# A long convolution with a mixture of experts: when the rows are ranked and scattered

## The chip, the cores and the metric

The kernel runs on one core of a Trainium2 chip. The metric is the device time of one execution in microseconds, as the median of the runs. One further execution was profiled; rows of the profile are from that one.

## The reference

The program first convolves and then routes. For each of 4 batches of 10048 rows with 128 channels:

```python
h_filt = (np.maximum(pos_emb @ w1, 0.0) @ w2) * window
y = irfft(rfft(x * v, n=2 * S) * rfft(h_filt, n=2 * S))[:, :S]
x = (x * y).reshape(B * S, D)          # 40192 rows of 128
```

Each row then chooses one of 4 groups (the largest of `x @ w_group`) and one of 4 experts in it (the largest of `x @ w_expert[g]`). It goes through that expert alone, with the product of the two softmax weights as its factor:

```python
out[row] = g_w * e_w * (np.maximum(x[row] @ w1[g, e], 0.0) @ w2[g, e])
```

## The kernel before

The convolution is a discrete Fourier transform written as matrix products on TensorE (PE). For batch `b` there are two stages.

- The *way in* forms `x * v`, folds it (`product`, `fold`, on VectorE) and transforms it in 43 steps of three channels (`dft_blocks`, matmuls `psa`, evicted to `z` by ScalarE). Between these steps stand the inverse transforms of the batch before (`turned`, `inverse_blocks`: matmuls `pt` and `po`, evictions `tt` and `oo` on ScalarE, `yt` and `xy` on VectorE).
- The *middle* runs over 40 pairs of frequencies. Each step is a matmul `psb` (`dft_positions`), the product with the filter's spectrum (two VectorE operations `t`, L629 and L632, then two halves of `y` on GpSimd, L630 and L633), and five steps later a matmul `pbp` from `y` back into `z` (`back`, evicted by ScalarE, L648).

W1, W2, W3 are the ways in of batches 1 to 3, each with the inverse of the batch before; M1, M2, M3 are the middles that follow them. A last way in holds the inverse of batch 3 alone. After it comes the experts' stage (`moe`).

What was convolved is routed meanwhile. `conv` drives a generator `routing` with `next(routing, None)`: 22 pieces of `chosen` (transpose rows, multiply by the router's weights, choose), then the pieces of `ranked`, which count the rows of each expert and compute a place `adr` in a sorted table `prow` for each row. In M1 batch 0 is chosen and its ranking begins, and so on. A pair of lists hands work to GpSimd's DMA queue: `self.scatters` gets 8 *clears* (L373, they need `fidx`, which the ranking computes early) and then 79 *scatters* of 128 rows each (L358, they need `adr`). `scatter(n)` issues up to `n` of them, not before three further calls have passed. Each waits for the latest eviction of the stage (`self.pace`). `between` and `beyond` tie a scatter's or a clear's place on GpSimd to the L633 around it: the L633 of the next step stands behind it. `stage` loads the rows that scatters send, `stg`, on SP's queue. The expert's stage needs the table, so scatters left over are issued there.

The order of instructions on each engine is set by a list scheduler at build time, which moves work past other work where dependencies allow. In the middles, `scatter` is called with 1 in three of four steps, and `next(routing)` in three of four steps up to the 30th and in every second one after it; in the ways in `next(routing)` is called after every second step, and `scatter` with 1 or 2.

Of the kernel before, what the change touches and what calls it, by code (L numbers as in the profile page):

```python
# [46 lines left out]
LAGS = 3  # L47
UB, STG = 4, 4
SAHEAD = 1
EVERY = 2  # L50
LATER = 48
CHOSEN = -(-NB // 4) + 2
# [72 lines left out]
def bc(ap, axis, n):  # L125

    ap = ap.unsqueeze(axis)
    shape = list(ap.shape)
    shape[axis] = n
    return ap.broadcast_to(shape)  # L130
# [9 lines left out]
class Kernel:  # L140
# [5 lines left out]
    def emit(self):  # L146
        tc, nc, d = self.tc, self.nc, self.d
        with ExitStack() as ctx:
            cp = ctx.enter_context(tc.tile_pool(name="const", bufs=1))
            self.ident = cp.tile([128, 128], F32, name="ident")  # L150
            make_identity(nc, self.ident)
            st = ctx.enter_context(tc.tile_pool(name="state", bufs=1))
            self.rem = st.tile([128, NE], F32, name="rem")
            self.cur = st.tile([128, NE], F32, name="cur")
            self.used = st.tile([128, 1], F32, name="used")
            for t in (self.rem, self.cur, self.used):
                nc.vector.memset(t, 0.0)
            pg = self.pages
            pg.epg = st.tile([128, pg.hp], F32, name="epg")
            pg.epgi = [st.tile([1, hi - lo], I32, name=f"epgi{lo}") for lo, hi in pg.parts]  # L160
            pg.count = st.tile([1, 1], I32, name="count")
            nc.vector.memset(pg.epg, 0.0)
            self.entries = ctx.enter_context(tc.tile_pool(name="entries", bufs=2))
            self.empty = st.tile([128, ZR, RW], F32, name="empty")
            nc.vector.memset(self.empty, 0.0)
            nc.vector.memset(self.empty[:, :, 128], BIGID)
            self.units, self.staged, self.tick, self.sent = [], 0, 0, None
            self.minus, self.pace = {}, None
            self.all = [Page(self, q) for q in range(pg.n)]
            self.w = [None, None]  # L170
            with ExitStack() as right:
                rout = ExitStack()
                self.rp = rout.enter_context(tc.tile_pool(name="rout", bufs=1, reuse_waits="tile"))
                with ExitStack() as c2:
                    routing = self.conv(c2, right)
                with ExitStack() as c2:
                    self.moe(c2, right, routing)
                rout.close()
# [22 lines left out]
    def conv(self, ctx, right):  # L201
# [26 lines left out]
        for b in range(self.nbat + 1):  # L228
            last = b == self.nbat
            if last:  # L230
                ahead.close()
                inner.close()
                self.sp = ctx.enter_context(tc.tile_pool(name="stream", bufs=2, reuse_waits="tile"))
                weights = self.first_weights(right)
                xy = self.z.rearrange("p k s d -> p (k s) d")[:, :NB]
            elif b > 0:
                xy = xyp.tile([128, NB, D], F32, tag="xy", name=f"xy{b - 1}")
            parts = groups(D, GD) if not last else []
            if b == 1:
                self.router_consts()  # L240
            self.run_ahead(b, 0, made, folded)
            for j, (d0, n) in enumerate(OUTS):
                if b > 0 and j % 2 == 0:
                    tts = self.turned(d0, min(2 * GI, D - d0))
                for i in range(2 * j, min(2 * j + 2, len(parts))):
                    self.run_ahead(b, i, made, folded)
                    self.scatter(1 + (i >= 12 and i % 2))
                    self.dft_blocks(*folded[i])
                    if b > 0 and i % 2 == 0:
                        self.inverse_blocks(b - 1, xy, d0, n, tts)  # L250
                if last:
                    self.inverse_blocks(b - 1, xy, d0, n, tts)
                    next(weights, None)
                    if j == 8:
                        self.scatter(sum(1 for s in self.scatters if s[0] < self.nbat - 2))
                        for p in self.all[:XG]:
                            p.load()
                for _ in range(3 if last else 1):
                    next(routing, None)
                if last:  # L260
                    self.scatter(1 + j % 2)
            made, folded = [], []
            if b > 0:
                oh = self.rp.tile([128, NE, NB], F32, tag="oh", name="oh")
                en = self.entries.tile([128, NB, 2], F32, tag="en", name="en")
                routing = chain(self.chosen(b - 1, xy, oh, en), self.ranked(b - 1, oh, en))
                if last:
                    for _ in range(CHOSEN):
                        next(routing)
            if not last:  # L270
                back = []
                for i, (k0, n) in enumerate(groups(NB, 2)):
                    back.append(self.middle(b, k0, n))
                    if len(back) > LAG:
                        self.back(*back.pop(0))
                    if b == 1 and i % 4 == 1:
                        self.clear_rest(i // 4)
                    self.scatter(i % 4 != 3)
                    if i % 4 != 3 if i < 30 else i % 2:
                        next(routing, None)  # L280
                for args in back:
                    self.back(*args)
        return routing
# [26 lines left out]
    def scatter(self, n):  # L310
        self.tick += 1
        for _ in range(min(n, len(self.scatters))):
            b, send, tick, u = self.scatters[0]
            if u:
                self.stage(u.k)

            if tick > self.tick and n < NB:
                break
            ins = send()
            self.between(ins)  # L320
            if self.pace is not None:
                kind = mybir.DependencyInfo(mybir.DependencyClass.Sync, mybir.DependencyReason.DATA)
                self.tc.add_manual_dep(ins.ins, self.pace.ins.name, kind, reason="one step at a time")
            self.scatters.pop(0)

    def unordered(self, ins, group, *others):
# [57 lines left out]
    def dft_blocks(self, b, eo, d0, n, other=False):  # L384
# [13 lines left out]
            self.z[:, :NB, :, d0 : d0 + n].rearrange("p k s d -> p (k s) d"),  # L398
            ps[:, :n].rearrange("p d c -> p c d"),
        )  # L400
        self.pace = ins
        self.in_turn(b, ins)
        self.tc.declare_no_dep(ins.ins, group=f"z{b}", reason="every step has channels of its own")
        self.tc.add_to_no_dep_group(f"z{b}", ins.ins)
# [231 lines left out]
    def back(self, k0, n, bp, y):  # L636

        nc = self.nc
        po = self.psT.tile([128, 2, 2, 128], F32, tag="pt", name="pbp")
        for i in range(n):  # L640
            nc.tensor.matmul(  # L641
                po[:, i].rearrange("p s d -> p (s d)"),
                bp[:, i],
                y[:, i].rearrange("p s d -> p (s d)"),
                start=True,
                stop=True,
            )
        self.pace = nc.scalar.copy(self.z[:, k0 : k0 + n], po[:, :n])  # L648

    def turned(self, d0, n):  # L650

# [25 lines left out]
    def inverse_blocks(self, b, xy, d0, n, tts):  # L677
# [35 lines left out]
        nc.scalar.activation(oo[0:64], by_row[64:128], AF.Copy, scale=-1.0)  # L713
        ins = nc.scalar.copy(oo[64:128], by_row[0:64])
        if b == self.nbat - 1:
            self.pace = ins
        pool, tag, bufs = (self.ap, "y", NY) if b < self.nbat - 1 else (sp, "yt", 2)
        yt = rows(pool.tile([128, GI * NB], F32, tag=tag, name="yt", bufs=bufs))
        nc.vector.tensor_tensor(yt, by_row, oo, ALU.add)
# [113 lines left out]
    def ranked(self, b, oh, en):  # L833
# [72 lines left out]
        c1, thr, dlt = small("c1"), small("thr"), small("dlt")  # L906
        v.tensor_tensor(c1, pre, base, ALU.add)
        v.tensor_scalar(c1, c1, -1.0, None, ALU.add)
        v.tensor_tensor(thr, self.rem, base, ALU.add)
        v.tensor_tensor(dlt, self.cur, base, ALU.subtract)  # L910
        if tail:
            thr2, dlt2 = small("thr2"), small("dlt2")
            v.tensor_scalar(thr2, fend, float(TP), None, ALU.mult)
# [4 lines left out]
        for h in range(4):  # L918
# [5 lines left out]
            v.tensor_tensor(first, first, c1[:, es], ALU.add)  # L924
            v.tensor_tensor_scan(flat(f), flat(self.keep), flat(oh[:, es]), 0.0, ALU.mult, ALU.add)
            v.tensor_tensor(first, first, c1[:, es], ALU.subtract)
            if h % 2:
                yield
            lt = rp.tile([128, 4, NB], F32, tag="big2", name="lt")
            w = v if b >= self.nbat - 2 or h < 2 else nc.gpsimd  # L930
            v.tensor_tensor(lt, f, bc(thr[:, es], 2, NB), ALU.is_lt)
            if fine and h % 2:
                yield
            w.tensor_tensor(lt, lt, bc(dlt[:, es], 2, NB), ALU.mult)
            if h % 2:
                yield
            w.tensor_tensor(f, f, lt, ALU.add)
            if tail:

                v.tensor_tensor(lt, f, bc(thr2[:, es], 2, NB), ALU.is_ge)  # L940
                if h % 2:
                    yield
                w.tensor_tensor(lt, lt, bc(dlt2[:, es], 2, NB), ALU.mult)
                w.tensor_tensor(f, f, lt, ALU.add)
# [6 lines left out]
            v.tensor_reduce(other, f.rearrange("p e t -> p t e"), AX.X, ALU.add)  # L951
            if h:
                v.tensor_tensor(pos, pos, other, ALU.add)
            if h % 2:
                yield
        v.memset(pos[64:128, NB - 1 : NB], BIGID)
        adr = self.entries.tile([128, NB], I32, tag="adr", name="adr")
# [79 lines left out]
    def moe(self, ctx, right, routing):  # L1037
# [9 lines left out]
        self.pst = ctx.enter_context(tc.tile_pool(name="pst", bufs=1, space=PSUM, reuse_waits="tile"))  # L1047
        self.psr = lambda shape, name: self.pst.tile(shape, F32, tag="pt", name=name)
        pg = self.pages
        self.routing, self.fix, self.pace = routing, tc.keep_in_program_order, None  # L1050
        self.outs, self.spare, self.owed, self.part = [], 0.0, 0.0, 0.0
        self.work(self.all[: pg.usual])
        if pg.usual < pg.n:
# [370 lines left out]
```

## Time and profile before

| | us |
|---|---|
| median of 3 runs | 2085.32 |
| lowest and highest run | 2081.45, 2090.16 |
| the profiled execution | 2083.48 |
| its span in the trace | 2081.7 |
| TensorE busy in it | 1962.0 (94%) |
| VectorE, ScalarE, GpSimd busy | 1626.1, 1444.8, 1333.4 |

The span is the time from the first to the last instruction. A busy share is a mean over stages with different limits, so the stages are to be read one by one. The convolution takes about the first half of the span, the experts' stage the second. In the rows, PE is TensorE, PEld its load of weights, DVE VectorE, ACT ScalarE, POOL GpSimd; a name like L633 is a line of the program.

### The profile page before, as it was taken

The numbers are of one execution on the slowest core, as the hardware profiler recorded it, in microseconds if no ns is written. First come the engines' busy times: TensorE is split into PE (matmuls) and PEld (weight loads), VectorE is DVE, ScalarE is ACT, GpSimd is POOL, SyncE is SP. The second block draws the span as 40 slices with busy tenths as digits, with TensorE's granted clock in tenths as the row PEclk, the third lists the DMA queues.
The fourth block names the chain that finished last, engine by engine and source line by source line (L and its number), as shares of the span: only waits on it lengthen the run. The fifth ranks groups of instructions, "written<-read, shape, count | busy, mean of one in ns | idle before, by whom it ended". The sixth has DMA issues, their size and how long they took to land.

```text
span 2081.7 us, 54011 instructions
## 1 busy us (share of the span) xinstructions
PE 1962.0 (94%) x18062; PEld 1803.8 (87%) x18062; DVE 1626.1 (78%) x3432; ACT 1444.8 (69%) x3210; POOL 1333.4 (64%) x1371
## 2 busy tenths in 40 slices
PE   8988999979999789989899999999999999999997
PEld 7867888767787578768699999999999999999997
DVE  5587765687658765796599998889999998888885
ACT  6652477436753466436688788888888888888886
POOL 3157600665689657976357677888888886555554
PEclk9999999999999799999899999999999999999999
DMA  4699965976889578968544455555555554443442
GB/s 136 226 263 267 275 168 160 333 226 174 229 301 296 157 190 254 339 198 277 188 126 136 134 154 151 155 180 169 157 161 155 161 150 131 125 134 121 127 126 66
DMA packets 258721, 388.93 MB, mean 187 GB/s; under 512 B 32680, under 2 KB 132627, under 8 KB 258433
## 3 DMA queue, kind: packets, MB, share of 16 engines
q1 hardware_dynamic: 225024, 318.01, 50.8%
q0 software_dynamic: 23904, 51.83, 7.0%
q10 hardware_dynamic: 9504, 15.54, 2.8%
q8 instruction: 146, 2.39, 0.5%
q14 instruction: 143, 1.16, 0.2%
HBM read 303.24 MB, written 83.04 MB: 186 GB/s over the span
## 4 chain that ended last, share of the span: by engine, by line
PE 50%; DVE 2%; POOL 2%; issue 1%; DMA 1%; ACT 0%; SPq 0%; DVEq 0%; ACTq 0%; POOLq 0%
PE py L1293 7%; PE py L1291 7%; PE py L1292 7%; PE ph L1272 7%; PE ph L1274 7%; PE ph L1273 7%; PE ptm L1305 2%; PE px L1229 2%; POOL wl L1261 1%; POOL out L1317 1%; PE pt L671 1%; PE ptr L786 1%; PE po L696 0%; PE po L704 0%; DMA mw<-m_w 0%
## 5 line engine op out<-in xcount | busy, mean ns | idle before, releaser
L1281 DVE SCALAR_TENSOR_TENSOR hl<-ph,hh 128x512 fp32r<-128x512 f32 x656 | 445.2, 683 | 93.3 <-ACT hh L1280 92.5
L1280 ACT ACTIVATE hh<-ph 128x512 fp32r<-128x512 f32 x656 | 395.6, 603 | 138.8 <-PE ph L1274 71.9
L358 POOL DMA_INDIRECT prow<-stg,adr x316 | 355.1, 1124 | 136.4 <-issue 63.6
L1317 POOL DMA_INDIRECT out<-os,to x328 | 349.0, 1064 | 91.6 <-issue 72.5
L1291 PE MATMUL py<-hh,wh 128*128 128x256 f32 x1312 | 398.7, 304 | 0.0
L1272 PE MATMUL ph<-xh,wh 128*128 128x256 f32 x1312 | 373.5, 285 | 5.4 <-ACT wh L1254 2.8
L1293 PE MATMUL py<-hh,wl 128*128 128x256 f32 x1312 | 373.2, 284 | 5.5 <-POOL wl L1261 5.5
L1274 PE MATMUL ph<-xh,wl 128*128 128x256 f32 x1312 | 373.4, 285 | 0.4 <-DVE wl L1261 0.4
L1273 PE MATMUL ph<-xl,wh 128*128 128x256 f32 x1312 | 372.9, 284 | 0.0
L1292 PE MATMUL py<-hl,wh 128*128 128x256 f32 x1312 | 371.4, 283 | 0.0
L1261 POOL TENSOR_TENSOR wl<-ws,wh 128x512 fp32r<-128x512 f32 x162 | 220.1, 1359 | 202.1 <-ACT wh L1254 200.9
L1293 PEld LDWEIGHTS py<-hh,wl 128*128 128x128 f32 x1312 | 251.4, 192 | 8.4 <-POOL wl L1261 8.4
L1272 PEld LDWEIGHTS ph<-xh,wh 128*128 128x128 f32 x1312 | 252.8, 193 | 6.1 <-ACT wh L1254 3.0
L1274 PEld LDWEIGHTS ph<-xh,wl 128*128 128x128 f32 x1312 | 253.1, 193 | 0.9 <-DVE wl L1261 0.8
L1273 PEld LDWEIGHTS ph<-xl,wh 128*128 128x128 f32 x1312 | 253.2, 193 | 0.1
L1292 PEld LDWEIGHTS py<-hl,wh 128*128 128x128 f32 x1312 | 252.8, 193 | 0.0
L1291 PEld LDWEIGHTS py<-hh,wh 128*128 128x128 f32 x1312 | 252.0, 192 | 0.0
L1261 DVE TENSOR_TENSOR wl<-mw,wh 128x512 fp32r<-128x512 f32 x328 | 238.1, 726 | 0.0
L648 ACT COPY z<-pbp 128x512 f32<-128x512 f32 (+1 forms) x160 | 92.6, 579 | 207.1 <-PE pbp L641 204.2
L630 POOL TENSOR_TENSOR y<-t 128x256 f32<-128x256 f32 (+1 forms) x160 | 121.2, 757 | 159.5 <-DVE t L629 153.9
L471 PE MATMUL psb<-z,bt 128*128 128x256 f32 x790 | 201.1, 387 | 8.6 <-DMA bt<-c_b 2.8
L1254 ACT CAST wh<-mw 128x512 fp32r x328 | 206.6, 630 | 0.0
(232 smaller groups left out, 4339.7 us busy)
## 6 DMA issues: line engine op xcount, KB each, us to landing
ws<-m_w SPq DMA_DIRECT2D x328, 256.0 KB
ht<-hspec SPq DMA_DIRECT2D x156, 256.0 KB
xv<-xv_in SPq DMA_DIRECT2D x131, 288.0 KB
bt<-c_b SPq DMA_DIRECT2D x95, 256.0 KB
xg<-prow SPq DMA_DIRECT2D x164, 130.0 KB
bp<-c_bp SPq DMA_DIRECT2D x76, 256.0 KB
stg<-xyd SPq DMA_DIRECT2D x76, 256.0 KB
xyd<-xy SPq DMA_DIRECT2D x57, 256.0 KB
```

Source lines behind the costliest of these rows:

```text
L358: ins = self.nc.gpsimd.indirect_dma_start(self.d["prow"], bass.IndirectOffsetOnAxis(ap=u.adr[:, t : t + 1], axis=0), u.rows[:, t - u.t0], ...
L1254: k.fix(k.nc.scalar.copy(hi, self.matrix(i, half, self.ea)))
L1261: ins = v.tensor_tensor(lo, self.matrix(i, half, self.ed), self.wh[i][half].bitcast(F32), ALU.subtract)
L1272: k.fix(nc.tensor.matmul(ph[:, j], wh, self.xh, start=True, stop=False))
L1273: k.fix(nc.tensor.matmul(ph[:, j], wh, self.xl, start=False, stop=False))
L1274: k.fix(nc.tensor.matmul(ph[:, j], wl, self.xh, start=False, stop=True))
L1280: k.fix(nc.scalar.activation(hh, ph, AF.Relu))
L1281: k.fix(nc.vector.scalar_tensor_tensor(hl, ph, 0.0, hh.bitcast(F32), ALU.max, ALU.subtract))
L1291: k.fix(nc.tensor.matmul(self.py, wh, self.hh[c], start=(c == 0), stop=False))
L1292: k.fix(nc.tensor.matmul(self.py, wh, self.hl[c], start=False, stop=False))
L1293: k.fix(nc.tensor.matmul(self.py, wl, self.hh[c], start=False, stop=(c == NC - 1)))
L1317: ins = k.nc.gpsimd.indirect_dma_start(k.d["out"], bass.IndirectOffsetOnAxis(ap=self.to[:, h : h + 1], axis=0), o[:, h], None, bounds_chec ...
```

## The change

Five edits go together. In the way in, `scatter` is called with 2 at each step. In the middle, `next(routing)` is called at every step, so the 22 pieces of the choice take the first 22 steps and the ranking follows in the other 18. The ranking gets a `yield` at places where it had one in every second part (for all batches but the last). A scatter or clear waits for the eviction before the latest (`BEHIND`), not for the latest. For batch 0, for which `rem` and `cur` are zero, the comparison with `thr` and what follows from it are left out.

```diff
-            self.minus, self.pace = {}, None
+            self.minus, self.pace = {}, []
...
-                    self.scatter(1 + (i >= 12 and i % 2))
+                    self.scatter(2)
...
                     self.scatter(i % 4 != 3)
-                    if i % 4 != 3 if i < 30 else i % 2:
-                        next(routing, None)
+                    next(routing, None)
...
-            if self.pace is not None:
+            if len(self.pace) >= BEHIND:
...
-                self.tc.add_manual_dep(ins.ins, self.pace.ins.name, kind, reason="one step at a time")
+                self.tc.add_manual_dep(ins.ins, self.pace[-BEHIND].ins.name, kind, reason="step by step")
...
-        v.tensor_tensor(thr, self.rem, base, ALU.add)
-        v.tensor_tensor(dlt, self.cur, base, ALU.subtract)
+        if b:
+            v.tensor_tensor(thr, self.rem, base, ALU.add)
+            v.tensor_tensor(dlt, self.cur, base, ALU.subtract)
...
-            if h % 2:
+            if h % 2 or not fine:
                 yield
             lt = rp.tile([128, 4, NB], F32, tag="big2", name="lt")
             w = v if b >= self.nbat - 2 or h < 2 else nc.gpsimd
-            v.tensor_tensor(lt, f, bc(thr[:, es], 2, NB), ALU.is_lt)
-            if fine and h % 2:
-                yield
-            w.tensor_tensor(lt, lt, bc(dlt[:, es], 2, NB), ALU.mult)
-            if h % 2:
-                yield
-            w.tensor_tensor(f, f, lt, ALU.add)
+            if b:
+                v.tensor_tensor(lt, f, bc(thr[:, es], 2, NB), ALU.is_lt)
+                if fine and h % 2:
+                    yield
+                w.tensor_tensor(lt, lt, bc(dlt[:, es], 2, NB), ALU.mult)
+                if h % 2 or not fine:
+                    yield
+                w.tensor_tensor(f, f, lt, ALU.add)
```

`BEHIND` is 2, `fine` is true for the last batch alone, and the two later places with `if h % 2:` get the same `or not fine`.

The edits move instructions on every engine. On GpSimd, at the end of M3 before the change, the last halves of `y` alternate with scatters; the clears (`prow<-empty,fidx`) come behind the first `z` of the last way in:

```order
L358 DMA prow<-stg,adr 52224x130
L630 TENSOR_TENSOR y<-t_11887 128x2x128
L633 TENSOR_TENSOR y<-t_11890 128x2x128
L358 DMA prow<-stg,adr 52224x130
L630 TENSOR_TENSOR y<-t_11905 128x128
L633 TENSOR_TENSOR y<-t_11908 128x128
L358 DMA prow<-stg,adr 52224x130
L721 TENSOR_TENSOR z<-yt,xo 128x79x6
L350 COPY stg<-en 128x4x2
L358 DMA prow<-stg,adr 52224x130 x2
L373 DMA prow<-empty,fidx 13056x520
```

After the change the clears of M3 stand some ten steps ahead of its end (the number behind `t_` rises with the step):

```order
L630 TENSOR_TENSOR y<-t_11675 128x2x128
L630 TENSOR_TENSOR y<-t_11699 128x2x128
L633 TENSOR_TENSOR y<-t_11702 128x2x128
L630 TENSOR_TENSOR y<-t_11722 128x2x128
L630 TENSOR_TENSOR y<-t_11748 128x2x128
L630 TENSOR_TENSOR y<-t_11769 128x2x128
L373 DMA prow<-empty,fidx 13056x520
L633 TENSOR_TENSOR y<-t_11678 128x2x128
L373 DMA prow<-empty,fidx 13056x520
L633 TENSOR_TENSOR y<-t_11725 128x2x128
L373 DMA prow<-empty,fidx 13056x520
L633 TENSOR_TENSOR y<-t_11751 128x2x128
```

Four L633, those of `t_11678`, `t_11725`, `t_11751` and `t_11772`, now stand behind the first four clears, while the L630 of the same steps stand ahead of them.

On VectorE, at the end of M3 before the change (`t_11905` and `t_11908` are its last step), the ranking's small operations start beside the last `t`:

```order
L632 TENSOR_TENSOR t_11890<-psb,ht 128x512
L879 TENSOR_SCALAR one<-npg 128x16
L629 TENSOR_TENSOR t_11905<-psb,ht 128x256
L880 TENSOR_TENSOR npg<-npg,one 128x16
L893 TENSOR_SCALAR lastp<-one 128x16
L632 TENSOR_TENSOR t_11908<-psb,ht 128x256
L881 SCALAR_TENSOR_TENSOR fend<-ones,used,npg 128x16
L996 TENSOR_SCALAR tmp<-need 128x16
L999 TENSOR_TENSOR r_12094<-rem,tot 128x16
L882 SCALAR_TENSOR_TENSOR end<-ones,fend,one 128x16
L884 TENSOR_TENSOR start<-fend,npg 128x16
```

After the change ranking operations on whole tables (`f`, `lt`) stand between the `t` of the middle:

```order
L926 SCALAR_TENSOR_TENSOR f<-keep,oh 128x316
L925 TENSOR_TENSOR oh<-oh,c_11608 128x4
L971 TENSOR_REDUCE ec<-e_12061 128x2
L927 TENSOR_TENSOR oh<-oh,c_11608 128x4
L933 TENSOR_TENSOR lt<-f,thr 128x316
L632 TENSOR_TENSOR t_11798<-psb,ht 128x512
L936 TENSOR_TENSOR lt<-lt,dlt 128x316
L629 TENSOR_TENSOR t_11818<-psb,ht 128x512
L939 TENSOR_TENSOR f<-f,lt 128x316
L632 TENSOR_TENSOR t_11821<-psb,ht 128x512
L942 TENSOR_TENSOR lt<-f,thr_11615 128x316
L629 TENSOR_TENSOR t_11844<-psb,ht 128x512
```

The same operations have moved ahead of some seven steps of `t`.

On TensorE, at the end of M3 before the change, one `pbp` follows each `psb`:

```order
L471 MATMUL psb_11883<-z_103,bt_11879 128x256 x2
L641 MATMUL pbp_11893<-y_11797,bp_11791 128x256 x2
L471 MATMUL psb_11902<-z_103,bt_11879 128x256
L641 MATMUL pbp_11911<-y_11819,bp_11791 128x256 x2
L641 MATMUL pbp_11921<-y_11842,bp_11836 128x256 x2
L641 MATMUL pbp_11925<-y_11861,bp_11836 128x256 x2
L641 MATMUL pbp_11929<-y_11886,bp_11880 128x256 x2
L641 MATMUL pbp_11933<-y_11904,bp_11880 128x256
L661 MATMUL pt_11947<-ident_58,z_103 32x128 x12
```

After the change, at the place of the clears:

```order
L641 MATMUL pbp_11754<-y_11653,bp_11647 128x256
L471 MATMUL psb_11765<-z_103,bt_11740 128x256 x2
L471 MATMUL psb_11791<-z_103,bt_11787 128x256 x2
L471 MATMUL psb_11814<-z_103,bt_11787 128x256 x2
L471 MATMUL psb_11840<-z_103,bt_11836 128x256 x2
L641 MATMUL pbp_11775<-y_11674,bp_11647 128x256 x2
L641 MATMUL pbp_11801<-y_11698,bp_11692 128x256 x2
L641 MATMUL pbp_11824<-y_11721,bp_11692 128x256 x2
L641 MATMUL pbp_11850<-y_11747,bp_11741 128x256 x2
L471 MATMUL psb_11861<-z_103,bt_11836 128x256 x2
L641 MATMUL pbp_11871<-y_11768,bp_11741 128x256 x2
```

Behind `psb_11765` three more `psb` now stand ahead of `pbp_11775`, whose `y_11674` is made by the L633 of `t_11678`.

## Rows read from the trace of the kernel before

**Rows 1.** Busy us of PE, PEld, DVE, ACT, POOL; clock, DMA, GB/s, by stretch

```profile
255.00:360.00 105.00, 100.24 (x1516) 88.80 (x1516) 65.12 (x116) 81.59 (x163) 0.00 (x0) 1.00 0.57 160
471.00:585.00 114.00, 104.10 (x1509) 91.70 (x1507) 71.41 (x146) 79.77 (x160) 71.34 (x72) 0.96 0.73 202
701.00:822.00 121.00, 109.00 (x1526) 94.42 (x1524) 80.47 (x174) 82.08 (x162) 77.37 (x74) 0.93 0.69 194
...
360.00:471.00 111.00, 99.85 (x652) 79.53 (x650) 85.87 (x199) 45.57 (x107) 73.21 (x92) 0.95 0.85 274
585.00:701.00 116.00, 100.99 (x645) 78.52 (x643) 91.28 (x195) 44.45 (x104) 98.83 (x119) 0.93 0.86 283
822.00:924.00 102.00, 94.68 (x589) 73.93 (x585) 81.45 (x179) 40.19 (x93) 92.55 (x119) 0.98 0.81 276
1052.00:2082.00 1030.00, 1008.86 (x8422) 1004.27 (x8420) 888.10 (x1846) 858.38 (x1938) 738.11 (x663) 0.99 0.47 142
```

**Rows 2.** Last 30 evictions of each way in (min/median/max ns, first, last); scatters

```profile
L397 ACT COPY z<-psa x30: 437/636/749, 288.9 to 360.0; 128x474 f32<-128x474 f32 x29, 128x316 f32<-128x316 f32 x1
...
L397 ACT COPY z<-psa x30: 430/639/748, 511.2 to 584.9; 128x474 f32<-128x474 f32 x29, 128x316 f32<-128x316 f32 x1
...
L397 ACT COPY z<-psa x30: 430/630/740, 741.8 to 821.5; 128x474 f32<-128x474 f32 x29, 128x316 f32<-128x316 f32 x1
...
L358 POOL DMA_INDIRECT prow<-stg,adr x44: 976/988/2609, 510.1 to 585.8; - x44
```

**Rows 3.** Evictions L648: plain steps (first middle), steps with choice (second)

```profile
L648 ACT COPY z<-pbp x15: 586/586/587, 207.1 to 231.2; 128x512 f32<-128x512 f32 x15
...
L648 ACT COPY z<-pbp x23: 567/586/588, 371.5 to 426.9; 128x512 f32<-128x512 f32 x23
```

**Rows 4.** Who PE waited for, 360:471, 585:701, 822:924; us, times, longest

```profile
PE pbp L641 <- POOL y L633: 9.3, 2, 7.8
...
PE pbp L641 <- POOL y L633: 11.6, 7, 7.0
...
PE pbp L641 <- POOL y L633: 5.5, 6, 1.5
```

**Rows 5.** The same, stretches 471:585, 701:822 and 924:1001

```profile
PE pt L671 <- ACT tt L673: 9.8, 8, 3.7
...
PE pt L671 <- ACT tt L673: 12.0, 7, 3.8
...
PE po L696 <- DVE yt L719: 3.0, 3, 1.3
```

**Rows 6.** Timeline 449:460, start and us; in brackets idle time before

```profile
451.44 0.46 POOL L630 TENSOR_TENSOR y<-t 128x128 f32<-128x128 f32 x1 [0.52 <-DVE start L887]
...
454.35 1.61 POOL L373 DMA_INDIRECT prow<-empty,fidx  x1 [2.46 <-DVE oh L924]
...
455.95 2.44 POOL L633 TENSOR_TENSOR y<-t 128x256 f32<-128x256 f32 x1
...
458.44 2.07 PE L641 MATMUL pbp<-y,bp 128*128 128x256 f32 x4 [7.82 <-POOL y L633]
...
458.55 1.33 POOL L373 DMA_INDIRECT prow<-empty,fidx  x1 [0.17 <-issue]
...
459.90 0.75 POOL L633 TENSOR_TENSOR y<-t 128x256 f32<-128x256 f32 x1
```

**Rows 7.** Timeline 683:697, the same columns

```profile
688.50 4.74 POOL L633 TENSOR_TENSOR y<-t 128x128 f32<-128x128 f32 x1
...
689.85 0.47 DVE L937 TENSOR_TENSOR f<-f,lt 128x316 f32<-128x316 f32 x1
...
693.29 1.22 PE L641 MATMUL pbp<-y,bp 128*128 128x256 f32 x2 [6.95 <-POOL y L633]
```

**Rows 8.** Groups of VectorE, 180:930; busy us, mean ns, idle before

```profile
L632 DVE TENSOR_TENSOR t<-psb,ht 128x512 f32<-128x512 f32 x154 | 104.9, 681 | 3.8 <-POOL y L630 3.7
...
L934 DVE TENSOR_TENSOR lt<-lt,dlt 128x316 f32<-128x316 f32 x5 | 2.8, 562 | 0.0
```

More of the change, by code (lines that the diff above doesn't have):

```diff
@@ L49 @@
 SAHEAD = 1
+BEHIND = 2
 EVERY = 2
@@ L400, in dft_blocks @@
         )
-        self.pace = ins
+        self.pace.append(ins)
         self.in_turn(b, ins)
@@ L647, in back @@
             )
-        self.pace = nc.scalar.copy(self.z[:, k0 : k0 + n], po[:, :n])
+        self.pace.append(nc.scalar.copy(self.z[:, k0 : k0 + n], po[:, :n]))
     def turned(self, d0, n):
@@ L715, in inverse_blocks @@
         if b == self.nbat - 1:
-            self.pace = ins
+            self.pace.append(ins)
         pool, tag, bufs = (self.ap, "y", NY) if b < self.nbat - 1 else (sp, "yt", 2)
@@ L930, in ranked @@
             w = v if b >= self.nbat - 2 or h < 2 else nc.gpsimd
-            v.tensor_tensor(lt, f, bc(thr[:, es], 2, NB), ALU.is_lt)
-            if fine and h % 2:
-                yield
-            w.tensor_tensor(lt, lt, bc(dlt[:, es], 2, NB), ALU.mult)
-            if h % 2:
-                yield
-            w.tensor_tensor(f, f, lt, ALU.add)
+            if b:
[6 more added lines that the diff above has]
+                w.tensor_tensor(f, f, lt, ALU.add)
             if tail:
                 v.tensor_tensor(lt, f, bc(thr2[:, es], 2, NB), ALU.is_ge)
-                if h % 2:
+                if h % 2 or not fine:
                     yield
@@ L953, in ranked @@
                 v.tensor_tensor(pos, pos, other, ALU.add)
-            if h % 2:
+            if h % 2 or not fine:
                 yield
@@ L1049, in moe @@
         pg = self.pages
-        self.routing, self.fix, self.pace = routing, tc.keep_in_program_order, None
+        self.routing, self.fix, self.pace = routing, tc.keep_in_program_order, []
         self.outs, self.spare, self.owed, self.part = [], 0.0, 0.0, 0.0
```

## Prediction

> **What bounds the kernel now.** I read the busy windows by stage first, then TensorE's waits in each stage, then the timeline of the two longest of those waits. [rows 1]: the experts' stage (1052 to 2082) has TensorE busy for 1008.86 of 1030 us; nothing that the change moves can shorten it, so the change is decided between 255 and 1052. There the stages alternate. W1, W2 and W3 (ways in of batches 1, 2 and 3: forward transform of one batch, inverse of the batch before) take 105, 114 and 121 us for the same matmuls; M1, M2 and M3 (the middles behind them, with the change of stage) take 111, 116 and 102. W1 carries neither ranking nor scatters. So W2 and W3 pay 9 and 16 us for these, and the middles pay something too: TensorE waits there for GpSimd's `y`, for 9.3, 11.6 and 5.5 us [rows 4]. In W2 and W3 it waits for ScalarE's `tt` instead, for 9.8 and 12.0 us [rows 5].
>
> The reader should see how M1's long wait comes about [rows 6]. The ranking writes `fidx` on VectorE. The first clear needs it, waits 2.46 us for VectorE and starts at 454.35. Second halves of `y` (L633) stand behind that clear on GpSimd, and TensorE, whose `pbp` needs such a `y`, stands idle for 7.82 us. Behind it clears (1.33 us) and `y` (0.75 us) alternate. M2 shows the same with another cause on top [rows 7]: a half-size `y`, 0.46 us in [rows 6], takes 4.74 us while VectorE runs operations such as `f<-f,lt` back to back, and TensorE idles for 6.95 us. M3 has no such hold: its clears come after its last `y`.
>
> A step of a middle costs TensorE 24.1/14 = 1.72 us when it carries no choice of experts (207.1 to 231.2), and 55.4/22 = 2.52 us on average when three of four steps carry one [rows 3]; so a choice is worth (2.52 - 1.72)/0.75 = 1.07 us and such a step lasts 2.79.
>
> **The change part by part.**
>
> *A choice at every step.* 20 groups of rows are chosen as before. TensorE's work in a middle is unchanged, 40 x 1.72 + 20 x 1.07 us before and after; what changes is that all the plain steps (some 18) now lie together at the end, with the ranking among them. GpSimd needs 2 x 0.75 us for `y` in a choice step of 2.79, so nothing there gets tighter. Price 0.
>
> *The ranking now runs in the middle.* The rows of the order show where. In M3 the chain to `fidx` used to start beside the last `t` and the ranking proper came after it; now some ten `t` pairs follow. GpSimd's order holds four L633 behind the first four clears, and TensorE's order puts three `psb` ahead of the first `pbp` that needs one. Three terms come from this.
>
> (a) The hold. Bounds per middle: 7.8 us, as in M1 [rows 6], if the wait is as long as there; 7.8 less the 2.2 us of extra `psb` that now stand ahead of it (three of 0.86, half a step's 1.72, against half of one in M1), so 5.6; and nothing if `fidx` is ready in time, which the order speaks against. I take 6, nearest to the second. M1 changes by 6 - 7.8 = -1.8, M2 by 6 - 7.0 = -1.0, M3 by +6. Sum +3.2.
>
> (b) The clears. All 8 now stand between `y`s that TensorE needs; before, 4 did in M1, 1 in M2 and none in M3. A plain step with a clear costs GpSimd 2 x 0.75 + 1.33 = 2.83 us against TensorE's 1.72, so a clear costs 1.1. M1: 4 x 1.1 and a little for the two products of the ranking that go to GpSimd, 4.9. M2: 7 x 1.1 = 7.7. M3: 8 x 1.1 = 8.8. On the other side the scatters leave M2 and M3. In choice steps they were hidden; in the plain steps they cost the short waits for `y`: 11.6 - 7.0 = 4.6 in M2 and 5.5 in M3 [rows 4]. Net 4.9, 3.1 and 3.3. Sum +11.3.
>
> (c) VectorE. A plain step needs two `t` of 0.68 us and now two or so operations of the ranking at some 0.56 [rows 8]: 2.5 us against 1.72. While clears run, GpSimd is slower still (2.83) and hides it; four or so steps without clears remain, 0.8 each, mostly hidden by the clears' backlog. Bounds 0 and 3.2 per middle; I take 1 for M2 and M3, 0 for M1, whose ranking is the shortened one. Sum +2.
>
> *The ways in.* W2 loses the whole ranking of batch 0 and gets nearly all of its 79 scatters, where about two thirds stood. What a scatter costs there is read from the last 30 evictions of each way in, where the ranking is over [rows 2]: 71.1 us in W1 without scatters, 73.7 in W2 with 44, so 2.6; in W3 79.7, of which the end of its ranking is a part. For 79 scatters 2.6 x 79/44 = 4.7 us; bounds 2.6 and 8.6. W2 becomes 105 + 4.7, a change of -4.3. W3 keeps the last two of four parts of batch 1's ranking, those whose products go to GpSimd and back: counting VectorE's instructions by the order, half of that time stays. Of its 16 us, 2.6 were scatters and 13.4 ranking; half of that is 6.7, with 4.7 for scatters 105 + 11.4 = 116.4, a change of -4.6. The last way in also loses part of a ranking; its only wait of TensorE for VectorE is 3.0 us [rows 5], so the bounds are 0 and -3; I take -1.
>
> *Pacing two steps back, and the steps' list.* Scatters wait for ScalarE, but nothing that TensorE needs stands behind them in a way in; in the middles the clears' wait gets easier. Price 0; without that cover the worst is what stands behind a clear, which (a) and (b) count. SP loads `stg` for 79 rows in one way in rather than in a way and a middle, 20 loads in either; its waits there are for `load` buffers, not for these. *Shorter ranking of the first batch*: 14 operations fewer, 4 of them on GpSimd, counted already in M1 and W2.
>
> **Sum.** +3.2 + 11.3 + 2 - 4.3 - 4.6 - 1 = +6.6 us. The profiled execution took 2083.48 us (span 2081.7), 1.84 under the median of the three runs, 2085.32; so 2083.5 + 6.6 = 2090. What TensorE's clock adds is in the waits' neighbourhood: its mean is 0.93 to 0.98 in the stages with long waits and 1.00 in W1 [rows 1]; since waits go in the ways and come in the middles, I leave it even.
>
> **Rivals.**
>
> *Faster: the hold is hidden.* In the middle's interior TensorE may have enough `psb` and earlier `pbp` ahead to bridge `fidx`. Then M1 and M2 win 7.8 and 7.0 and M3 pays nothing: 14.8 + 3.2 = 18.0 better than my sum, 2072. For it: the chain to `fidx` now runs while GpSimd has no scatter. Against it: the order, in which the `y` stands behind the clear. It decides if the wait of the first clear for VectorE, 2.46 us in [rows 6], is gone.
>
> *Slower: `y` is starved by the ranking.* The 4.74 us for 0.46 [rows 7] is one instruction; 2.44 instead of 0.75 [rows 6] is another. If in each middle two `y` lose between 1.7 and 4.3 us to runs of ranking operations, that is 10 to 26 us in all; at some 15, 2105. It decides if these operations run back to back; the order alternates them with `t`, which speaks against, save for the run just behind `fidx`. The Trainium skill ("SBUF — State Buffer", section "SBUF: two separate sides") says that a VectorE operation with two SBUF inputs and a GpSimd operation that reads SBUF hold a shared pair of ports exclusively, one instruction at a time; the trace agrees, with the 4.74 us. By that rule alone each ranking operation moved beside a `y` would add its own length.
>
> *Slower: GpSimd is full in the ways in.* Two scatters per step at 0.99 us and up (the median of the 44 in [rows 2]) and the copies for them stand against 105/43 = 2.44 us per step. If it lags, the first `y` of the next middle comes late, and so does M3, whose scatters run to the end of W3: some 8 us, 2098. Against it: nothing else runs on GpSimd there. It decides if the first `pbp` of M3 waits.
>
> **How the numbers follow.** Half a per cent, about 10 us, is what a measurement of this kernel can tell from no change: 2075 to 2096. My forecast has 0.45, with 2080 to 2100 as its own range; hidden hold 0.25; starved `y` 0.20; full GpSimd 0.10. The forecast lies within 0.5% for 0.40 of its 0.45; the first rival is faster for 0.23 of 0.25; the others are slower for 0.27 of 0.30. Faster 0.23, same 0.45, slower 0.32. The range runs from below the first rival, 2068, to above the second, 2108.
>
> **What would show it.** W2 at about 110 us and W3 at about 116; M1, M2 and M3 at about 114, 119 and 112; in each middle one wait of TensorE for `y` of about 6 us, ten steps ahead of the end, and steps of 2.8 us behind it with `y` and clears alternating on GpSimd. The prediction is wrong if the middles get shorter, if W2 or W3 stays as long as before, or if `y` at several microseconds turns up more than once in a middle.

## The result and the profile after

The changed kernel takes 2095.48 us (median of 9 runs, 2093.05 to 2101.04), the kernel before 2081.45 us (9 runs) on the same chip: a ratio of 1.0067, 95% interval 1.0049 to 1.0085, so 14 us slower. The forecast was 2090, with 2068 to 2108 as its range. The profiled execution's span grew from 2081.7 to 2093.6 us, by 11.9 where the sum said 6.6.

The stages of the changed kernel, as busy time of TensorE, its weight load, VectorE, ScalarE and GpSimd, then TensorE's clock (W1, M1, W2, M2, W3, M3, last way in):

```profile
255.00:363.00 108.00, 102.88 (x1534) 90.82 (x1533) 65.13 (x117) 82.17 (x163) 0.00 (x0) 0.98 0.57 159
363.00:485.00 122.00, 104.96 (x626) 79.89 (x626) 91.95 (x215) 44.12 (x102) 80.00 (x106) 0.92 0.78 253
485.00:597.00 112.00, 104.83 (x1518) 91.90 (x1515) 65.41 (x117) 79.60 (x162) 89.58 (x90) 0.95 0.83 234
597.00:715.00 118.00, 104.84 (x648) 79.84 (x646) 93.63 (x210) 44.77 (x104) 76.82 (x93) 0.93 0.79 255
715.00:833.00 118.00, 106.73 (x1519) 92.91 (x1516) 72.46 (x160) 81.12 (x162) 91.59 (x96) 0.94 0.78 220
833.00:946.00 113.00, 98.15 (x609) 74.22 (x609) 88.71 (x216) 40.60 (x94) 77.92 (x98) 0.97 0.73 242
946.00:1017.00 71.00, 68.86 (x1067) 59.03 (x1060) 35.01 (x70) 49.37 (x87) 41.72 (x45) 1.00 0.80 250
```

Against [rows 1] M1 is 11 us longer, M3 11, M2 2, W2 and W3 are 2 and 3 shorter. The last way in, from the end of M3's last eviction to the first transpose of the choice behind it (`ptr`), fell from 77.6 to 71.3 us. W1, in which the change moves nothing, is 1.9 us longer (104.7 to 106.6 between its first and last eviction; other traces of these kernels have 104 to 109), and the experts' stage, which the forecast left even, is 3.2 us shorter. Whom TensorE waited for (us in total, times, longest), in M1 (two rows), M2 and M3, then in W2 and W3:

```profile
PE pbp L641 <- POOL y L633: 8.3, 3, 4.3
PE psb L471 <- DVE t L632: 4.9, 3, 3.3
...
PE pbp L641 <- POOL y L633: 10.5, 6, 4.4
...
PE pbp L641 <- POOL y L633: 12.4, 9, 4.5
...
PE pt L671 <- ACT tt L673: 7.1, 6, 2.0
...
PE pt L671 <- ACT tt L673: 8.7, 6, 5.2
```

M3's waits for `y` rose from 5.5 to 12.4 us [rows 4]. In M1 and M2 they fell a little, and in M1 a wait for VectorE's `t` stands beside them. Lines from the timelines of GpSimd, TensorE and VectorE in M1 show three places (start, duration, in brackets the idle time before):

```profile
445.10 1.08 POOL L373 DMA_INDIRECT prow<-empty,fidx  x1 [2.59 <-DVE oh L925]
446.16 1.01 POOL L633 TENSOR_TENSOR y<-t 128x256 f32<-128x256 f32 x1
...
447.23 5.52 PE L641 MATMUL pbp<-y,bp 128*128 128x256 f32 x16 [3.50 <-POOL y L633]
...
451.60 0.69 DVE L632 TENSOR_TENSOR t<-psb,ht 128x512 f32<-128x512 f32 x1 [0.55 <-POOL y L633]
...
454.13 1.06 DVE L949 TENSOR_TENSOR f<-f,oh 128x316 f32<-128x316 f32 x1
...
456.16 0.78 DVE L955 TENSOR_TENSOR pos<-pos,other 128x79 f32<-128x79 f32 x1
456.86 1.33 DVE L926 TENSOR_TENSOR_SCAN f<-keep,oh 128x316 f32<-128x316 bf16 x1
...
458.18 0.68 DVE L629 TENSOR_TENSOR t<-psb,ht 128x512 f32<-128x512 f32 x1
...
459.67 1.13 PE L471 MATMUL psb<-z,bt 128*128 128x256 f32 x4 [3.27 <-DVE t L632]
...
467.75 1.00 POOL L373 DMA_INDIRECT prow<-empty,fidx  x1 [0.15 <-issue]
...
473.42 1.39 POOL L358 DMA_INDIRECT prow<-stg,adr  x1 [2.29 <-DMA xo<-x_out]
474.85 0.73 POOL L633 TENSOR_TENSOR y<-t 128x256 f32<-128x256 f32 x1
...
475.63 3.29 PE L641 MATMUL pbp<-y,bp 128*128 128x256 f32 x6 [4.26 <-POOL y L633]
```

First the hold, as in [rows 6] but 3.50 us long: the first clear waits for the ranking, the L633 stands behind it. Then, from 452.3 (the end of the `t` at 451.60) to 458.18, VectorE runs the ranking with no `t` in it, and TensorE finds no free `psb`. Last, the first scatter of rows waits 2.29 us, again with an L633 behind it. The profile puts this wait down to a load of `xo`, but the updates of that load's semaphore run on to 474.1, after the scatter has started. The scatter's own rows had been asked for at 409.4 (the first L347). The last clear, issued at 467.75, landed at 472.5; a row has to come behind the clears of its batch, so that landing is the likely end of the wait. No run tested it.

### The profile page after: what moved, and what is told of

Read it like the earlier page. It is cut to its first block, busy times and chain, and to the rows that moved or that the text cites. A ratio compares the mean times of both kernels' runs of the same rounds, so it can differ in the third digit from the quotient of the medians.

```text
span 2093.6 us, 54005 instructions
## 1 busy us (share of the span) xinstructions
PE 1970.3 (94%) x18062; PEld 1802.5 (86%) x18062; DVE 1615.1 (77%) x3422; ACT 1442.3 (69%) x3210; POOL 1327.8 (63%) x1367
## 4 chain that ended last, share of the span: by engine, by line
PE 73%; DMA 8%; DVE 6%; POOL 5%; ACT 3%; issue 3%; SPq 1%; ACTq 0%; DVEq 0%; POOLq 0%
PE py L1295 7%; PE py L1293 7%; PE py L1294 7%; PE ph L1276 7%; PE ph L1274 7%; PE ph L1275 7%; PE psb L471 6%; PE pbp L641 5%; DMA xv<-xv_in 4%; PE psa L392 4%; PE pt L671 2%; PE po L696 2%; PE po L704 2%; PE ptm L1307 2%; PE px L1231 2%
## 5 line engine op out<-in xcount | busy, mean ns | idle before, releaser
L630 POOL TENSOR_TENSOR y<-t 128x256 f32<-128x256 f32 (+1 forms) x160 | 121.6, 760 | 215.2 <-DVE t L629 207.2
L648 ACT COPY z<-pbp 128x512 f32<-128x512 f32 (+1 forms) x160 | 92.6, 580 | 230.8 <-PE pbp L641 229.3
```

## The experiments

The runs went to three chips: e1 to e4 to one, c1, e5, e9 and e1 again to the second, c0, e10, e11 and e12 to the third. On these the kernel before took 2132 to 2141 us, not 2081 as where the result was measured (called the first chip below; its number is not known), so every ratio is to the kernel before on the run's own chip. The stages, each from its own trace: a way in from the first `z` eviction to the last, a middle from there to the first eviction of the next way in (M3 to its last eviction), in us; and the scatters that start in W2 and W3 between these two evictions ("rows", of 128 rows each).

| kernel | M1 | M2 | M3 | W2 (rows) | W3 (rows) | ratio |
|---|---|---|---|---|---|---|
| before, first chip | 110.4 | 115.8 | 102.3 | 114.5 (49) | 120.8 (45) | |
| changed, first chip | 122.9 | 117.9 | 112.3 | 112.0 (73) | 117.8 (72) | 1.007 |
| before, again | 110.3 | 114.9 | 104.9 | 124.9 (50) | 130.7 (45) | |
| changed, again | 122.8 | 117.2 | 112.1 | 144.9 (73) | 153.2 (78) | 1.027 |
| e4 steps alone | 125.9 | 136.4 | 132.5 | 120.8 (57) | 119.0 (56) | 1.025 |
| e5 two per step alone | 110.3 | 112.4 | 105.8 | 152.3 (69) | 145.7 (61) | 1.019 |
| e3 old steps in M1 | 111.7 | 120.6 | 112.3 | 144.9 (62) | 154.7 (78) | 1.032 |
| e2 clears only | 118.3 | 116.1 | 100.6 | 146.6 (75) | 157.8 (78) | 1.031 |
| e1 again: changed, ways only | 111.6 | 105.7 | 99.6 | 155.9 (79) | 162.5 (79) | 1.031 |
| e9 before, ways only | 98.2 | 98.8 | 95.9 | 155.1 (72) | 155.9 (63) | 1.014 |
| e11 changed, 1.5 per step | 122.0 | 116.5 | 113.1 | 132.4 (61) | 129.5 (58) | 1.013 |
| e12 changed, no loads | 120.0 | 116.5 | 109.8 | 143.3 (73) | 152.3 (78) | 1.032 |
| e10 before, clears in the ways | 98.0 | 100.1 | 97.3 | 132.1 (52) | 135.8 (48) | 0.996 |

The middles repeat from chip to chip within some 3 us; the ways in do not. So the middles are compared across the whole table, and the ways in only among the later runs.

**e1, no clears and no rows in a middle.**

```diff
-                    self.scatter(2)
+                    self.scatter(2 + (i < 12))
...
-                    self.scatter(i % 4 != 3)
+                    self.scatter(0)
```

> The changed kernel, but no clear and no scatter is issued in a middle: all go to the ways in, three per step in the first twelve steps and two after. Theory A (what stands between the y on GpSimd, the clears and in M1 the first scatter, holds TensorE): the waits of TensorE for y, 8.3 us in M1, 10.5 in M2 and 12.4 in M3, go, M1 falls from 123 to some 112 us, M2 from 118 to 108, M3 from 112 to 102, and the time is about 2070. Theory B (the ranking on VectorE between the t costs the middles): M1 keeps its 4.9 us of waits for t, M2 and M3 take waits of TensorE for t in place of those for y, about 2090. Theory C (GpSimd is full in the ways in): 87 clears and scatters at 1.0 to 1.3 us fill 105 us, the first y of M2 and M3 come late by 5 us or more each, 2085 to 2095.

2215.71 us against 2138.36, 1.0369 (1.0319 to 1.042). M1, M2 and M3 were 113.3, 108.5 and 100.9 us, as theory A has it; of TensorE's waits for `y` some 3 us stayed in M1 and M2, and in M1 a wait for `t` of 3.9 us, as theory B has it. W2 and W3 took 157 and 168 us, far more than theory C's price, and the first `y` of M2 was not what waited: the evictions within the ways were slow.

**e2, clears only in a middle.**

```diff
-                    self.scatter(i % 4 != 3)
+                    self.scatter(i % 4 != 3 and bool(self.scatters) and self.scatters[0][3] is None)
```

> The changed kernel, but in a middle only clears are issued, no scatter of rows. In M1 the first scatter waited for its rows and TensorE for the y behind it, 4.3 us, and the clock fell after it. Theory A: that wait goes and a part of the half clock with it, M1 falls from 123 to 116 to 119 us, M2 and M3 stay at 118 and 112, about 2089. Theory B: M1 is long because of VectorE, the wait for y turns into one for t, and the time stays at 2095.

2201.6 us, 1.0307 (1.0258 to 1.0356). M1 fell to 118.3, so the first rows cost it 4.5 us, the length of TensorE's third wait above (4.26). What the first scatter waited for was not its rows, as said there. By M3 rows of batch 1 were left at the head of the list and kept the clears out of it: M3 is 100.6 us, 11.7 shorter than with its clears.

**e3, M1 at the steps of before.**

```diff
-                    next(routing, None)
+                    if b != 1 or (i % 4 != 3 if i < 30 else i % 2):
+                        next(routing, None)
```

> The changed kernel, but in the middle of batch 1 the choice and the ranking are called at the steps of before (M2 and M3 keep the new steps). If M1 is where the change loses (the traces have W1 and M1 together 14 us longer and the rest even): M1 falls from 123 to 109 to 112 us, W2 takes 2 us more, about 2083. Rival: the ranking of batch 0 then stands in W2 as before and costs its 4 us there, clears in M1 still hold TensorE as before (7.8 us), and the scatters of batch 0 reach into M2: 2090 to 2095.

2202.18 us, 1.0315 (1.026 to 1.037). M1 is 111.7 us, 11 shorter: it is the new steps that make it long, by where they put the ranking and the clears. The shorter ranking, its extra places to yield and the pacing, which e3 keeps, leave M1 within 1.3 us of the kernel before. What W2 gave back can't be read beside its slow rows.

**e4, the choice at every step alone.** In the kernel before:

```diff
-                    if i % 4 != 3 if i < 30 else i % 2:
-                        next(routing, None)
+                    next(routing, None)
```

> The kernel before with one edit alone: the choice and the ranking are called at every step of a middle. If these steps are what makes the change slow: slower than before by 14 us or more, since the scatters still stand in the middles too, M1 above 120 us with the unshortened ranking, 2095 to 2102. Rival: they are worth nothing or a gain (the ways lose their ranking), and two scatters per step or the spread ranking cost the 14 us: 2075 to 2084.

2188.18 us, 1.0254 (1.0206 to 1.0301): this edit by itself is slower by 50 us. Against the kernel before, again, M1, M2 and M3 grow by 16, 22 and 28 us, W2 and W3 fall by 4 and 12, although each has more rows.

**c1, the changed kernel again, and c0, the kernel before again**, both unedited.

> The changed kernel once more, beside the kernel before on the same chip. The three runs with two scatters per step had W2 at 145 to 157 us where the changed kernel's trace had 112, with TensorE's gaps put down to no release, and the kernel before took 2138 us there. If that is the chip: the changed kernel is 3% slower on such a chip and 0.7% on one where the kernel before takes 2081. If it is what the edits of those runs did: 0.7% on either.

> The kernel before once more, for its trace on a chip like those of the runs so far. If dense scatters are what such a chip is slow at: W2 and W3, with 52 and 48 scatters, at 116 to 124 us, the middles as in the first trace (110, 116, 102), the last way in and the experts' stage longer by 10 and 20 us, in all 2130. If such a chip is slow at scatters of any density: W2 and W3 above 130.

The changed kernel took 2195.92 us against 2131.99, 1.0274 (1.0224 to 1.0324), where the first chip had 1.0067: the same program loses four times as much here. The kernel before took 2147.34 us in its one run, the profiled one; its W2, 124.9, lies between the two cases expected, its W3, 130.7, at the second. For the same program the stages of the changed kernel on the later chip (the columns as above; M1, W2, M2, W3, M3):

```profile
364.00:487.00 123.00, 104.98 (x645) 80.17 (x643) 92.29 (x216) 44.24 (x104) 79.12 (x106) 0.92 0.79 253
487.00:632.00 145.00, 120.60 (x1520) 98.98 (x1518) 66.44 (x117) 79.97 (x163) 85.36 (x90) 0.92 0.66 182
632.00:749.00 117.00, 103.01 (x644) 78.34 (x642) 93.04 (x208) 44.40 (x102) 76.70 (x93) 0.94 0.78 254
749.00:902.00 153.00, 124.27 (x1513) 101.00 (x1511) 72.66 (x160) 79.57 (x161) 95.64 (x104) 0.91 0.62 177
902.00:1015.00 113.00, 99.72 (x610) 76.22 (x610) 87.92 (x212) 40.72 (x94) 71.83 (x91) 0.95 0.72 233
```

and TensorE's waits in its W2:

```profile
PE pt L671 <- issue: 6.6, 3, 4.6
PE po L704 <- issue: 6.1, 12, 1.1
PE pt L671 <- ACT tt L673: 5.6, 4, 1.7
PE psa L392 <- issue: 3.1, 8, 0.9
```

"issue" is a wait to which the profile gives no releaser. The trace of the first chip has none of these in W2. ScalarE and VectorE are as busy as there within 1 us, GpSimd 4 us less; TensorE's busy time is 16 us longer, its gaps 17.

**e9, the kernel before with nothing issued in a middle.** The edit is that of e1, with its steps of choice and ranking.

> The kernel before, with its own steps of choice and ranking, but no clear and no scatter in a middle: three per step in the first twelve steps of a way in, two after. Theory A: the middles lose their waits for y (9.3, 11.6 and 5.5 us), M1 falls from 110 to 102 us, M2 from 116 to 105, M3 from 102 to 98; W2 and W3 take 2 to 4 us more each for the scatters of before that stood in a middle, on a chip like the first: about 2066. Theory C, dense scatters slow the ways in by 30 us or more: 2120 and more.

2158.31 us, 1.0137 (1.0093 to 1.018). Its middles, M1 to M3:

```profile
357.50:455.70 98.20, 95.45 (x649) 77.27 (x646) 78.53 (x181) 44.08 (x103) 68.68 (x88) 1.00 0.87 281
611.00:710.00 99.00, 95.53 (x652) 77.42 (x654) 79.93 (x186) 44.24 (x103) 67.94 (x85) 1.00 0.84 268
865.00:961.00 96.00, 93.58 (x599) 74.71 (x595) 73.31 (x175) 40.19 (x93) 61.95 (x82) 0.98 0.77 248
```

The waits for `y` are gone, and the granted clock is 1.00, 1.00 and 0.98. The gain, 12, 17 and 6 us, is more than the waits named in [rows 4]. Theory C holds for the ways in on this chip.

**e1 again.**

> The changed kernel with no clear and no scatter in a middle, again, beside the changed kernel itself. On the chip of the first four runs the middles were short as theory A has it (113, 108 and 101 us against 123, 118 and 112) and the ways in were 157 and 168 us. If dense scatters stretch the ways on some chips only: about 2070 where the changed kernel takes 2095, and above the changed kernel where that takes 2200. If the clears in the way in did it: 2200 in either case.

2195.13 us, 1.0308 (1.0275 to 1.0341), equal to the changed kernel beside it (2195.92). In the two traces the middles are 35 us shorter and W2 and W3 20 us longer; the two profiled executions differ by 12 us, so what else the medians lost can't be read from them. The middles of this run, M1 to M3, have no clear and no scatter ahead of their last `y`:

```profile
364.00:475.00 111.00, 101.26 (x656) 78.39 (x653) 88.08 (x215) 44.34 (x102) 70.50 (x94) 0.97 0.81 260
632.00:737.00 105.00, 99.11 (x659) 77.22 (x660) 87.56 (x204) 43.80 (x102) 66.01 (x84) 0.98 0.80 259
900.00:1000.00 100.00, 94.66 (x601) 73.31 (x601) 82.69 (x200) 40.40 (x93) 61.73 (x81) 0.98 0.75 243
```

VectorE is busy for some 8 to 10 us more in each than in e9. Lines of its timeline in M1 show what stands in the way once the clears are gone, the last `t` before a row of ranking operations, the next `t`, and who waits for it:

```profile
446.08 0.68 DVE L632 TENSOR_TENSOR t<-psb,ht 128x512 f32<-128x512 f32 x1
...
451.80 0.67 DVE L629 TENSOR_TENSOR t<-psb,ht 128x512 f32<-128x512 f32 x1
...
452.55 0.73 POOL L630 TENSOR_TENSOR y<-t 128x256 f32<-128x256 f32 x1 [4.89 <-DVE t L629]
...
453.96 1.13 PE L471 MATMUL psb<-z,bt 128*128 128x256 f32 x4 [3.70 <-DVE t L632]
```

**e5, two per step alone.** In the kernel before:

```diff
-                    self.scatter(1 + (i >= 12 and i % 2))
+                    self.scatter(2)
```

> The kernel before with one edit alone: two scatters at each step of a way in. The middles then hold no rows but the last 15 of a batch, and the ranking stays where it was. If the choice at every step is what costs the 14 us: M2 falls by 3 to 5 us for its scatters, W2 and W3 grow by 2, 2075 to 2081. If two per step are the cost: slower than before by 10 us or more, in W2 and W3.

2175.12 us, 1.019 (1.0153 to 1.0227): W2 and W3 take 27 and 15 us more, and M2 only 2.5 us less. On a later chip this half of the change is a loss of its own.

**e11, 1.5 per step.**

```diff
-                    self.scatter(2)
+                    self.scatter(1 + i % 2)
```

> The changed kernel with 1.5 scatters per step in a way in, not 2, so that some 20 of each batch stand in the next middle. If it is the density that stretches the ways in: W2 falls from 145 to 120 to 125 us and W3 from 153 to 130, M2 and M3 grow by 4 us, some 2160 on a chip where the changed kernel takes 2196. If it is the number of scatters: 145 falls by a fifth of the 33 us, to 138.

2168.72 us, 1.0134 (1.0064 to 1.0204). W2 and W3 fall by 12 and 24 us for 12 and 20 scatters fewer (of 73 and 78). That is more than in proportion to the number; W2 misses the 120 to 125 us that density alone was to give, W3 reaches its 130. M2 and M3 take 13 and 21 rows and stay within 1 us.

**e12, the rows' loads left out.** Four fixed tiles of zeros are sent:

```diff
-            u.rows = self.entries.tile([128, UB, RW], F32, tag="stg", name="stg", bufs=STG)
...
-            ins = self.nc.sync.dma_start(u.rows[:, :n, 0:128], src[:, u.t0 : u.t0 + n])
-            if self.sent is not None:
-                self.after(ins, self.sent)
+            u.rows = self.fixed[self.staged % STG]
```

> The changed kernel without the loads of the rows that scatters send: the scatters send zeros from four fixed tiles (with the right numbers and factors), so the expert's rows are zero and SP's queue carries some 5 MB less per batch. If these loads, which go in pieces of 512 bytes, starve TensorE's instructions in the ways in: W2 falls from 145 us to 112 to 120. If the scatters themselves do it: W2 stays above 135. On a chip where the changed kernel's W2 is 112 it tells nothing.

2209.53 us, 1.0319 (1.0263 to 1.0376). W2 is 143.3 us: the loads are not what stretches it. What is left are the scatters and the small copies that go with them.

**e10, the clears out of the middles.** The kernel before, with 1.5 per step and:

```diff
-                    self.scatter(i % 4 != 3)
+                    rows = bool(self.scatters) and self.scatters[0][3] is not None
+                    self.scatter(i < 30 and i % 4 != 3 and rows)
```

> The kernel before with its steps of choice and ranking, 1.5 scatters per step in a way in, and in a middle rows only, in choice steps of the first 30; the clears go to the ways in. By the runs so far (M1 98 us, M2 99, M3 96 with nothing issued in a middle): M1 falls from 110 to 99 us, M2 from 116 to 101, M3 from 102 to 97, the ways in stay within 5 us: faster than before by 20 to 30 us on any chip. Rival: rows in choice steps are not free, or the clears stretch the ways: no change or slower.

2133.08 us against 2140.53, 0.9962 (0.9932 to 0.9991): the only version that beat the kernel before, by 7 us where 20 to 30 were expected. Its middles (98.0, 100.1, 97.3; 23 scatters in choice steps of M2 and M3 each, none in M1) are within 2 us of e9's, so rows there are nearly free. W2 and W3 took 7 and 5 us back, and W1, which carries nothing, was 109 us (104 to 109 in these runs). The two traces differ by 22 us, but this one is of the fastest of ten executions, and that of the kernel before is of one 7 us over its median. It was not run on the first chip.

## Why the prediction came out right, point by point

- **The middles lose, the ways win, and the loss is larger: right.** On the first chip M1, M2 and M3 change by +12.5, +2.1 and +10.0 (forecast +3.1, +3.1 and +10.3), W2 and W3 by -2.5 and -3.0 (forecast -4.3 and -4.6).
- **The sum came out near by luck.** Its terms (a) and (b) were some 14 us too dear, (c) some 22 us too cheap, the last way in 5 us too dear; so 6.6 stands against 11.9 in the traces and 14 between the medians.
- **(a) and (b), hold and clears: too dear.** The hold was 3.5, 4.4 and 4.5 us (in M2 and M3 the longest wait of TensorE for `y`), not 6. Behind it the clears of M2 start 2.0 to 5.1 us apart, where steps of 2.8 were forecast. Taking everything out prices both kernels: with the steps of before, clears and rows cost the middles 12.2, 17.0 and 6.4 us (before less e9), with the new steps 11.3, 12.2 and 12.7 (changed less e1 again; a middle repeats within 3 us, and no difference here is better than that). So these two terms came to -1, -5 and +6, together about 0, where the sum had +14.5. M2's loss before the change was under-read: its named waits are 11.6 us of the 17.0.
- **(c) VectorE: the mis-sized term.** The steps themselves, with nothing issued among the `y` of a middle, cost 13.4, 6.9 and 3.7 us (e1 again less e9), 24 together (with the shorter ranking, its yields and the pacing, which e1 keeps), where the sum had 0, 1 and 1. The evictions of `pbp` say where. From the end of the way in to the 34th of the 40, M1 takes 87.1 us in e1 and 87.0 in e9, M2 87.7 and 86.6: the choice at every step costs about nothing, as the sum had it. In M3 it is 87.6 and 90.0, where e9 has its first `y` late. The last six take 17.7, 12.3 and 12.0 us in e1, with ranking operations among their `t`, and 5.9 in each middle of e9. The prediction counted two operations at 0.56 us to a step and set M1 at 0, "whose ranking is the shortened one". In M1 scans of 0.8 us and more, sums of some 0.7 and a string of small operations follow one another: without clears VectorE runs no `t` from 446.8 to 451.8, GpSimd waits 4.89 us for one, and TensorE 3.70 (the lines of e1 again). TensorE's waits for `t` are there with clears (4.9 us in M1) and without (4.1). That clears hide it did not hold: M1 pays for both.
- So M2 and M3 came out on forecast because two errors cancelled; M1, where (c) was the far larger one, is 9 us above it. Of M1's 12.5 us the gaps of TensorE are 6; its mean clock fell from 0.95 [rows 1] to 0.92, at 5 us more busy time for the same matmuls. "I leave it even" was wrong for M1; the last way in has the opposite (1.00 now, 0.97 before, shorter by 6.3 us where -1 was taken).
- **The ways in: right on the first chip**, 112.0 and 117.8 us for 110 and 116; 73 scatters cost W2 5.4 us over W1, 0.07 each, where [rows 2] gave 0.06. On the later ones they are 145 and 153: the price of a scatter there, some 0.5 us, is not a property of the program alone.
- **The rivals.** Hidden hold: no, the first clear waited 2.59 us for VectorE. Starved `y`: no, the 4.74 us of [rows 7] did not come back; no L633 of the three middles lasts more than 1.74 us. Where it took 4.74 us, ranking operations alternated with products and folds of the next way in; now they alternate with `t`. GpSimd full in the ways in: on the first chip the rows ran 10 us over the end of W3 and the first `y` of M3 started 7.9 us behind that end (2.6 in M1 and M2), but the first `pbp` waited under 1 us; on the later chips the ways are what costs, but GpSimd is no busier there, so that is another mechanism.

## What to carry to other kernels

A stage whose engines interleave is priced better by a version with all the extra work taken out than by the waits that the profile names: here the named waits (26 us) were three quarters of the price (36). Count a moved chain's small operations and scans too, against the slack of the step that they move into. Work for an in-order queue belongs where nothing waits behind it; where its cost depends on its density, measure that on more than one chip.

## What the runs showed of the hardware

One program took 112.0 us for W2 on one chip and 144.9 on another, and 117.8 and 153.2 for W3; the middles agree within 1 us. The whole span differs by 107 us: W2 and W3 are 68 of them, the last way in 14 and the experts' stage 25, and both of these scatter rows too. Whether it is the chip or something else that differed between these executions was not tested; three later chips showed it, one earlier one did not.

On the later chips the time per scatter of a way in seems to grow with their density: over the 104 us of a W1 without rows, W2 is 41 us longer with 73 scatters at 2 per step (0.56 each) and 28 with 61 at 1.5 per step (0.47). With a W1 of 108.6 us, as in the first of these two traces, it is 0.50, so the growth is small beside the spread of W1. Leaving out the loads of the rows changed W2 and W3 by less than 2 us. The lost time of TensorE shows as gaps with no releaser (17 us in W2, none in the first trace) and as 16 us more busy time at a lower granted clock, 0.92 for 0.95; VectorE has 10 us of such gaps where the first trace has 1. Whether this is the supply of instructions, the writes of the rows or something else was not settled.
